# Unread TensorE products in the planner's gaps ahead of the first MoE, and four results in other rings

## The chip, the cores and the metric

The kernel runs on one core of one Trainium2 chip. The metric is the device time of one execution in microseconds; a run's figure is that of the core, and versions are compared by the median of several runs.

## The reference, cut to what matters

Three stages are computed one after the other, all in single precision.

```python
scores = where(causal, -1e9, q @ k.T / 8 + minimum(cum_k - cum_q, 0))   # 4 batches, 8 heads, 576 tokens, 64 wide
x = (exp(scores - max) / sum) @ v            # laid out as 2304 tokens x 512
h = x @ w_in                                 # 512 x 2048
x = (h * sigmoid(1.702 * h)) @ w_out         # 2048 x 512, the first MoE
P = balanced gate probabilities of x         # 8 experts, 8 rounds of row and column scaling
out = sum over e of P[:, e] * (relu(x @ w1[e]) @ w2[e])   # the second MoE, 1024 wide
```

Nothing that the change adds is part of this: its extra products are written to a PSUM tile that no instruction reads.

## The kernel before, in words

**Stages.** The attention works on 64 pieces, each a part of the queries of one head: scores (`sp` tiles), exponentials (`sm`), transposes (`tp`), a copy of the transposed probabilities (`pf`, later `ph` and `pl`), products with the values (`op`), and a division into token rows (`xg`), which are transposed again (`xtp`) into the input of the first MoE (`xh`, `xl`). Meanwhile the weights of the first MoE arrive in chunks (`st`), which ScalarE, GpSimd and VectorE turn into two parts each. The first MoE takes seven blocks of 256 tokens (`mm1`, `mm2`) and, at its end, the last two blocks together, 512 wide (`wide1`, `wide2`, lines 1174 to 1217): for every 128 of the 2048 hidden features, 12 products into `hp`, a tanh into `t`, a product by VectorE, a split into `gh` and `gl`, and 12 products into four accumulators `accw`. The second MoE follows with its experts.

**The rings.** `t`, `gh` and `gl` are rings of two buffers each in one pool (`mpool`). The same pool has a ring `st` of two larger buffers, the stages: `staged` (line 1398) hands them out to the early conversion of the second MoE's weights and of the first two x blocks (`early_x_part`, line 1490, names `xa` and `xb`). At the end of the first MoE, `wide2` scales the four accumulators into `xo` with ScalarE, takes the largest magnitude of each with VectorE, and sends each to DRAM (`x2_d`) by the SP queue. Before the change two buffers of the stages hold the four results, two in each.

**The planner.** The order of all instructions on all queues is not written out by hand. A planner in the kernel's own code (`Sequencer`, from line 61) keeps a clock for each engine, reckons a cost for every operation and a landing time for every transfer, and emits the instructions in the order in which they would run by that reckoning. Operations of TensorE are issued at once; those of the other engines are held until the planner's clock of TensorE reaches the time at which they could start, and then issued by rank, attention first and weight chunks last.

The loop from line 2104 makes one choice per pass. It asks six candidates when they could start: scaling of the values, a transpose of finished tokens, a value product, a transpose of probabilities, a score, the next piece of the first MoE. The first that could start now is emitted. If none could, the planner's clock of TensorE is set on, to the earliest of the six times or by 100 ns, whichever is less, and nothing is emitted.

**Unread products.** `fill(n)` (line 524) emits a product of n columns into the tile `unread`. At the start 14 of 512 columns are emitted (line 1937). Until the first piece of the first MoE (`at_first`, cleared in line 2039) there is also a rule on the share of busy time: `share()` (line 283) adds up what the planner has put on TensorE in the last stretch of its clock, of the constant length `WINDOW`, where products with single-precision stationary operands count for 0.36 of their cost, and divides by `WINDOW`. As long as that is under the constant `SHARE`, a product of 128 columns is emitted and the pass ends there, whether or not a candidate could have started. The planner reckons such a product at 128 / 2.4 + 2.7 = 56 ns. All operations are issued from line 357, so the profile's rows have that line and are told apart by their tiles; `unread<-mask` are the unread products.

Of the kernel before, what the change touches and what calls it, by code (L numbers as in the profile page):

```python
# [9 lines left out]
F32 = mybir.dt.float32  # L10
F32R = mybir.dt.float32r
# [18 lines left out]
def f32(ap):  # L30
    return ap.bitcast(F32)
# [9 lines left out]
SHARE = 0.55  # L41
# [357 lines left out]
def kernel(  # L399
# [12 lines left out]
    seq = Sequencer()  # L412
# [10 lines left out]
    TB1 = 256  # L423
# [33 lines left out]
    mpool = Pool(seq, p1.enter_context(tc.tile_pool(name="mpool", bufs=2, side=left, reuse_waits="tile")))  # L457
# [252 lines left out]
    def load_more():  # L710
        nonlocal n_qk
        while n_qk < min(len(heads), n_scored + 3 + N_KF if n_qk < H else n_prep + (3 if n_qk < 2 * H else 1)):
            if n_qk == H and n_s < 3 or n_qk == H + 2 and (n_s < 4 or auxpool.held()):
                return
            seq.rank = 1 if n_qk > 1 else 0
            load_qk(n_qk)
            n_qk += 1
            seq.rank = 1
            prep_next(n_scored)
            seq.rank = 0  # L720
# [93 lines left out]
    def can_vpow():  # L814
        if not vpows or n_s < 2:
            return never
        return max(seq.settled(vpows[0][1].tensor.name), seq.slot(ps_a, bank_tag("T")))
# [10 lines left out]
    def more_vpow():  # L828

        if due and not any(in_mpool(c) for c in range(n_conv, n_load)):  # L830
            begin_vpow(due.pop(0), 0, 3, 1)

    def more_v():

        nonlocal n_pv
        seq.rank = 1 if n_v else 0
        while n_pv < min(len(heads), (units[n_v][0] if n_v < NU else 0) + 2):
            b, h = extent(n_pv)[0:2]
            if n_pv < N_F:
                v3_of[n_pv] = [x[:, h] for x in (vf if n_pv >= H else vf[0:2])]  # L840
                n_pv += 1
                continue
            if (b, h) not in scaled:
                break
            if n_pv not in va_of:
                load_v(n_pv)
            prep_v(n_pv)
            n_pv += 1
            load_v(n_pv)
        seq.rank = 0  # L850
# [201 lines left out]
    def can_turn():  # L1052
        if n_t >= n_s or n_t >= n_v + 2:
            return never
        return max(seq.slot(ps_a, bank_tag("T")), seq.settled(live[n_t][0].tensor.name))
# [27 lines left out]
    def try_finish():  # L1083

        nonlocal n_fin
        while n_fin < len(heads) and (n_v == NU or units[n_v][0] > n_fin):
            g, h = heads[n_fin]
            if h == 0:
                olds = xgs.get(g - 1, [])[:1] + (xgs.get(g - 2, [])[1:] if g % 2 else [])
                if any(x[0].tensor.name == o.tensor.name for q in pieces.values() for x in q for o in olds):  # L1090
                    return
            finish(n_fin)
            n_fin += 1

    def can_flush():
        for j in (k for k in sorted(xtile) if k < NB1):
            if pieces[j]:
                return max(seq.slot(ps_a, bank_tag("T")), seq.settled(pieces[j][0][0].tensor.name))
        return never
# [91 lines left out]
    def wide2():  # L1191
        p, i, gh, gl = pend.pop(0)
        first, last = (p, i) == (NPAIR - 1, 0), (p, i) == (0, 1)
        if first:
            accs[NB1 - 1] = [
                pool.tile([128, 2, TB1], F32, tag=tag, name="accw")
                for pool, tag in ((ps_m, "acc0"), (ps_m, "acc1"), (mem["ps"], "D"), (mem["ps"], "E"))
            ]
        acc = accs[NB1 - 1]
        for m in range(KC):  # L1200
            d = slice(m * 128, (m + 1) * 128)
            for n, (w, x) in enumerate(((woh[p], gh), (woh[p], gl), (wol[p], gh))):
                nc.tensor.matmul(acc[m], lhsT=w[:, i, d], rhs=x, start=(first and n == 0), stop=(last and n == 2))
            if last:
                if m % 2 == 0:
                    both = staged("xo")
                xo = both[:, m % 2 * 512:m % 2 * 512 + 512].rearrange("p (a t) -> p a t", a=2)
                nc.scalar.activation(out=xo, in_=acc[m], func=ACTF.Copy, scale=0.5 / gain**2)
                c = 2 * (NB1 - 2) + m
                nc.vector.tensor_reduce(  # L1210
                    out=xmx[:, c:c + 1], in_=xo, axis=AX.XY, op=ALU.max, apply_absolute_value=True,
                )
                nc.sync.dma_start(
                    out=x2_d[-1][:, m, TB1:], in_=xo.rearrange("p a t -> p (a t)")
                )
# [17 lines left out]
    def convert():  # L1233

        nonlocal n_load, n_conv
        c = n_conv
        if c == len(chunks) or sum(x.rank == 2 for x in seq.held["DVE"]) > ASKED:
            return
        if n_s == 0:
            return  # L1240
        seq.rank = 2
        while n_load < len(chunks) and way(n_load)[0] is not None and way(n_load)[2] < c:
            conv_load(n_load)
            n_load += 1
        seq.rank = 0
        if c == 4 * NP0 and stage[0] is spool:
            if n_s < NU and units[n_s][0] < 2 * H - 2 or n_v < NU and units[n_v][0] < 2 * H - 2:
                return
            if min(n_pv, n_prep) < 2 * H or spool.held() or spool2[0].held():
                return  # L1250
            su.close()
            alloc_w(Pool(seq, p1b.enter_context(
                tc.tile_pool(name="wpool1", bufs=1, side=left, reuse_waits="tile")
            )), range(NP0, NP1))

            stage[0] = Pool(seq, su.enter_context(
                tc.tile_pool(name="stage", bufs=1, side=left, reuse_waits="tile")
            ))
        if c == 4 * NP1 and NP1 not in wih:
            if stage[0].held():  # L1260
                return
            su.close()
            alloc_w(Pool(seq, p1b.enter_context(
                tc.tile_pool(name="wpool2", bufs=1, side=left, reuse_waits="tile")
            )), range(NP1, NPAIR))
        seq.rank = 2
        conv(c)
        n_conv += 1
        seq.rank = 0
# [128 lines left out]
    def staged(name):  # L1398
        return mpool.tile([128, 1024], F32, tag="st", name=name, bufs=2)
# [676 lines left out]
    def more_scales():  # L2076
        nonlocal firsts, first_of
        if n_conv < len(chunks):
            return
        if firsts is None:  # L2080
            firsts = first_scales()
        elif first_of is None:
            return
        elif isinstance(first_of, int):
            if n_out < first_of:
                return
        elif first_of is vpows:
            if vpows:
                return
        elif seq.settled(first_of.tensor.name) > seq.free["PE"]:  # L2090
            return
        seq.rank = 2
        first_of = next(firsts, None)
        if hasattr(first_of, "send"):
            vpows.append((first_of, next(first_of)))
            first_of = vpows
        seq.rank = 0

    wgs = None
    at_first = [True]  # L2100
# [3 lines left out]
    while moe1_can is not None:  # L2104
        convert()
        try_finish()
        load_more()
        more_vpow()
        more_v()
        more_scales()  # L2110
        seq.run()
        now = seq.free["PE"]
        if not seq.rough and n_pv >= 2 * H:
            seq.rough = True
        for seq.slack in (0,) if seq.rough else (SLACK, 0):
            times = [can_vpow(), can_flush(), can_value(), can_turn(), can_score(), moe1_can()]
            which = next((k for k, x in enumerate(times) if x <= now), None)
        if at_first and seq.share() < SHARE:
            fill(128)
            continue  # L2120
            if which is not None:
                break
        seq.slack = 0
        if which is None:
            stuck += 1
            assert stuck < 3000
            seq.free["PE"] = min(min(times), now + 100)
            continue
        stuck = 0
        if which < 5:  # L2130
            (do_vpow, do_flush, do_value, do_turn, do_score)[which]()
        else:
            moe1_can = next(moe1, None)
# [4 lines left out]

    qs, pq = {}, {}
    wide2()  # L2140
    while first_of is not None:
        seq.free["PE"] += 100
# [155 lines left out]
    while upcoming or any(active):  # L2298
# [8 lines left out]
        now = seq.free["PE"]  # L2307
# [11 lines left out]
        if best is None:  # L2319
            t = min(t for _, t, _ in ready)  # L2320
# [62 lines left out]
```

## Time and profile before

| | us |
|---|---|
| median of 3 runs | 1974.06 |
| lowest and highest of them | 1973.75, 1977.65 |
| the profiled execution, device time | 1970.51 |
| its span, first to last instruction | 1968.8 |

The span is the time between the first and the last instruction of the profiled execution; its device time includes what lies around that. The profile's busy time of an engine counts the time in which an instruction of it runs. In the timeline a row is a merged run of like instructions: start, duration, engine, line, operation, tile written and tiles read, count, and in brackets the idle time before it and what ended that.

### The profile page before, as it was taken

The numbers are of one execution on the slowest core, as the hardware profiler recorded it, in microseconds if no ns is written. First come the engines' busy times: TensorE is split into PE (matmuls) and PEld (weight loads), VectorE is DVE, ScalarE is ACT, GpSimd is POOL, SyncE is SP. The second block draws the span as 40 slices with busy tenths as digits, with TensorE's granted clock in tenths as the row PEclk, the third lists the DMA queues.
The fourth block names the chain that finished last, engine by engine and source line by source line (L and its number), as shares of the span: only waits on it lengthen the run. The fifth ranks groups of instructions, "written<-read, shape, count | busy, mean of one in ns | idle before, by whom it ended". The sixth has DMA issues, their size and how long they took to land.

```text
span 1968.8 us, 41111 instructions
## 1 busy us (share of the span) xinstructions
PE 1948.9 (99%) x15766; PEld 1565.4 (80%) x15766; DVE 1477.7 (75%) x3424; ACT 1237.4 (63%) x2553; POOL 111.2 (6%) x174
## 2 busy tenths in 40 slices
PE   8999999999999999999999999999999999999999
PEld 6899999999987777777777777777777777777777
DVE  7997888887655787887868877766777877776556
ACT  6877676676545776665666766656666666665333
POOL 1120000000000000000010000111110000111000
PEclk9999999999999999999999999999999999999999
DMA  7564454443247653565575575576748547566331
GB/s 235 176 203 151 121 145 142 112 137 102 74 116 257 230 177 118 196 220 191 197 205 158 132 235 156 125 201 180 196 117 253 153 133 210 155 154 185 121 132 44
DMA packets 230101, 322.13 MB, mean 164 GB/s; under 512 B 38272, under 2 KB 156224, under 8 KB 229904
## 3 DMA queue, kind: packets, MB, share of 16 engines
q1 hardware_dynamic: 216944, 295.90, 46.1%
q0 software_dynamic: 12960, 23.60, 8.5%
q8 instruction: 124, 2.03, 0.4%
q14 instruction: 73, 0.60, 0.1%
HBM read 230.85 MB, written 84.34 MB: 160 GB/s over the span
## 4 chain that ended last, share of the span: by engine, by line
PE 83%; DVE 6%; ACT 5%; DMA 1%; issue 1%; SPq 0%; ACTq 0%; DVEq 0%
PE C L357 17%; PE A L357 16%; PE D L357 16%; PE hp L357 9%; PE B L357 8%; PE acc L357 6%; PE sp L357 2%; ACT h L357 2%; PE op L357 2%; PE tp L357 2%; PE accw L357 2%; DVE h L357 2%; PE accx L357 1%; DVE hst L357 1%; DVE sa L357 1%; ACT w1o L357 1%
## 5 line engine op out<-in xcount | busy, mean ns | idle before, releaser
L357 PEld LDWEIGHTS <-h 128*128 128x128 f16 x6048 | 591.6, 98 | 85.1 <-issue 6.9
L357 PEld LDWEIGHTS <-w1o 128*128 128x128 f16 x4036 | 394.5, 98 | 253.6 <-issue 2.5
L357 PE MATMUL C<-xt,w1o 128*128 128x384 f16 x1152 | 218.6, 326 | 1.2 <-DVE hst L357 1.2
L357 PE MATMUL D<-xt,w1o 128*128 128x384 f16 x1152 | 218.4, 326 | 0.0
L357 PE MATMUL D<-w2o,h 128*128 128x256 f16 x1728 | 217.5, 273 | 0.2 <-DMA xt<-xc_d 0.2
L357 PE MATMUL A<-xt,w1o 128*128 128x384 f16 x1152 | 214.5, 326 | 0.0
L357 PE MATMUL A<-w2o,h 128*128 128x256 f16 x1728 | 212.3, 273 | 1.9 <-ACT B L357 1.6
L357 PE MATMUL C<-w2o,h 128*128 128x256 f16 x1728 | 208.4, 273 | 1.7 <-DVE y L357 1.5
L357 DVE SCALAR_TENSOR_TENSOR h<-hst,h 128x768 f16<-128x768 f32 (+1 forms) x192 | 138.7, 752 | 56.6 <-ACT h L357 56.5
L357 ACT COPY C<-B 128x384 f32<-128x384 f32 (+1 forms) x168 | 71.4, 425 | 154.1 <-PE B L357 91.6
L357 PE MATMUL hp<-xh,wih 128*128 128x256 f32 (+1 forms) x512 | 154.6, 302 | 0.7 <-DVE t L357 0.7
L357 PE MATMUL hp<-xl,wih 128*128 128x256 f32 (+1 forms) x512 | 151.4, 296 | 0.0
L357 PE MATMUL hp<-xh,wil 128*128 128x256 f32 (+1 forms) x512 | 151.2, 295 | 0.0
L357 POOL DMA_DIRECT2D acc_d<-y x90 | 78.0, 867 | 1220.5 <-DVE y L357 660.8
L357 ACT ACTIVATE h<-hst 128x768 f16<-128x768 f32 (+1 forms) x192 | 126.3, 678 | 3.8 <-DVE hst L357 3.7
L357 ACT ACTIVATE sm<-sm,stats 64x576 f32<-64x576 f32 (+4 forms) x160 | 94.7, 603 | 40.9 <-DVE stats L357 39.4
L357 PE MATMUL acc<-gh,woh 128*128 128x256 f32 x384 | 111.4, 290 | 0.0
L357 PE MATMUL B<-w2o,h 128*128 128x256 f16 x864 | 110.3, 273 | 0.0
L357 PE MATMUL B<-xt,w1o 128*128 128x384 f16 x576 | 109.3, 326 | 0.0
L357 PE MATMUL acc<-gl,woh 128*128 128x256 f32 x384 | 108.4, 282 | 0.0
L357 PE MATMUL acc<-gh,wol 128*128 128x256 f32 x384 | 108.3, 282 | 0.0
L357 ACT COPY B<-A 128x384 f32<-128x384 f32 (+1 forms) x168 | 70.2, 425 | 60.2 <-PE A L357 59.6
(239 smaller groups left out, 3865.7 us busy)
## 6 DMA issues: line engine op xcount, KB each, us to landing
xt<-xc_d SPq DMA_DIRECT2D x168, 384.0 KB
wm<-in_moe_w_dram SPq DMA_DIRECT2D x112, 256.0 KB
w2o<-w_d SPq DMA_DIRECT2D x56, 512.0 KB
wr<-in_moe_w_dram SPq DMA_DIRECT2D x112, 256.0 KB
w_d<-wo SPq DMA_DIRECT2D x98, 256.0 KB
acc_d<-y POOLq DMA_DIRECT2D x90, 256.0 KB, 5.1
kq<-in_qk_dram SPq DMA_DIRECT2D x32, 448.0 KB
st<-in_moe_w_in_dram SPq DMA_DIRECT2D x16, 512.0 KB
```

The costliest lines, as they stand in the source:

```text
L357: self.seq.submit(self.name, what, lambda: method(*args, **named), outs, ins, "accum_op" in named)
```

## The change

The condition under which an unread product is emitted ahead of the first MoE gets a second case: no candidate could start now (`which is None`), and the earliest of the six times is more than 60 ns ahead. The old case stays. And the four results of the last two blocks no longer take the stages: the first two take buffers of the ring `t`, the third one of `gh`, the fourth one of `gl`, the latter two read and written as plain single precision. The lines after `continue` can't be reached, before or after.

```diff
@@ -1202,9 +1202,10 @@
             for n, (w, x) in enumerate(((woh[p], gh), (woh[p], gl), (wol[p], gh))):
                 nc.tensor.matmul(acc[m], lhsT=w[:, i, d], rhs=x, start=(first and n == 0), stop=(last and n == 2))
             if last:
-                if m % 2 == 0:
-                    both = staged("xo")
-                xo = both[:, m % 2 * 512:m % 2 * 512 + 512].rearrange("p (a t) -> p a t", a=2)
+                if m < 2:
+                    xo = mpool.tile([128, 2, TB1], F32, tag="t", name="xo", bufs=2)
+                else:
+                    xo = f32(mpool.tile([128, 2, TB1], F32R, tag=("gh", "gl")[m - 2], name="xo", bufs=2)[:, :, :])
                 nc.scalar.activation(out=xo, in_=acc[m], func=ACTF.Copy, scale=0.5 / gain**2)
                 c = 2 * (NB1 - 2) + m
                 nc.vector.tensor_reduce(
@@ -2115,7 +2116,7 @@
         for seq.slack in (0,) if seq.rough else (SLACK, 0):
             times = [can_vpow(), can_flush(), can_value(), can_turn(), can_score(), moe1_can()]
             which = next((k for k, x in enumerate(times) if x <= now), None)
-        if at_first and seq.share() < SHARE:
+        if at_first and (seq.share() < SHARE or which is None and min(times) > now + 60):
             fill(128)
             continue
             if which is not None:
```

## Rows read from the trace of the kernel before

**Rows 1.** The page, part 1: busy us, share of the span and count by engine.

```profile
PE 1948.9 (99%) x15766; PEld 1565.4 (80%) x15766; DVE 1477.7 (75%) x3424; ACT 1237.4 (63%) x2553; POOL 111.2 (6%) x174
```

**Rows 2.** Windows by stage: busy us (count) of PE, PEld, DVE, ACT, POOL; clock; DMA; GB/s.

```profile
2.40:43.26 40.86, 37.23 (x288) 29.21 (x288) 32.46 (x111) 25.94 (x53) 6.64 (x21) 1.00 0.87 255
43.26:633.00 589.74, 584.14 (x5202) 543.67 (x5201) 468.79 (x1385) 387.64 (x797) 24.82 (x54) 1.00 0.48 144
633.00:1940.00 1307.00, 1301.97 (x10052) 969.88 (x10052) 964.26 (x1907) 818.95 (x1697) 77.99 (x90) 1.00 0.58 172
```

**Rows 3.** Timeline of TensorE ahead of the first MoE: start, us, instruction, idle before.

```profile
9.84 0.92 PE L357 MATMUL sp<-kf 66*128 66x128 f32 x4 [0.21 <-DVE stats L357]
10.60 1.34 PE L357 MATMUL unread<-mask 128*128 128x128 bf16 x21
11.77 0.82 PE L357 MATMUL tp<-ident,sm 128*128 128x128 f32 x6
...
15.36 1.00 PE L357 MATMUL unread<-mask 128*128 128x128 bf16 x15
17.58 0.88 PE L357 MATMUL op<-vf,pf 128*128 128x65 f32 x6 [1.22 <-ACT pf L357]
...
21.14 0.88 PE L357 MATMUL op<-vf,pf 128*128 128x65 f32 x6 [0.70 <-ACT pf L357]
21.86 0.61 PE L357 MATMUL unread<-mask 128*128 128x128 bf16 x8
...
23.06 0.89 PE L357 MATMUL unread<-mask 128*128 128x128 bf16 x13
...
24.68 0.44 PE L357 MATMUL tp<-ident,sm 128*128 128x128 f32 x2 [0.30 <-DMA two<-one]
...
27.92 0.42 PE L357 MATMUL sp<-two 68*128 68x384 f32 x1 [0.63 <-DMA two<-aux_d]
...
29.25 0.44 PE L357 MATMUL unread<-mask 128*128 128x128 bf16 x5
29.90 0.35 PE L357 MATMUL sp<-one 128*64 128x288 f32 x1 [0.21 <-DVE stats L357]
...
35.55 0.67 PE L357 MATMUL unread<-mask 128*128 128x128 bf16 x9
36.39 1.05 PE L357 MATMUL tp<-ident,sm 64*128 64x64 f32 x8 [0.17 <-DVE xl L357]
37.28 0.22 PE L357 MATMUL unread<-mask 128*128 128x128 bf16 x1
```

**Rows 4.** Timeline of ScalarE, 16 to 21 us.

```profile
16.50 0.67 ACT L357 ACTIVATE st<-st 128x512 f32<-128x512 f32 x1 [0.65 <-DMA st<-in_moe_w_in_dram]
17.07 0.46 ACT L357 COPY pf<-tp 128x384 f32<-128x384 f32 x1
...
19.77 0.94 ACT L357 CAST one<-kq 128x896 fp32r<-128x896 f32 x1 [1.54 <-DMA kq<-in_qk_dram]
```

**Rows 5.** Timeline of TensorE at the first MoE's last unit.

```profile
630.31 0.50 PE L357 MATMUL accw<-gl,woh 128*128 128x512 f32 x1 [0.68 <-DVE gl L357]
630.64 0.40 PE L357 MATMUL accw<-gh,wol 128*128 128x512 f32 x1
```

**Rows 6.** Timelines of the SP queue, VectorE and ScalarE around the four results.

```profile
619.17 10.75 SPq L357 DMA_DIRECT2D xc_d<-xb  x7
...
629.57 0.68 DVE L357 TENSOR_TENSOR gl<-t,gh 128x512 fp32r<-128x512 f32 x1
...
631.08 2.65 ACT L357 ACTIVATE xo<-accw 128x512 f32<-128x512 f32 x4 [2.00 <-PE accw L357]
```

**Rows 7.** Windows of TensorE alone: length, busy us (count), granted clock, DMA share, GB/s.

```profile
2.40:8.15 5.75, 5.75 (x14) 1.00 0.40 113
...
17.00:18.00 1.00, 0.42 (x4) 1.00 0.79 269
18.00:25.00 7.00, 6.00 (x59) 1.00 1.01 271
```

## The prediction, made before the change was run

> **What bounds the kernel now.** I read the page's busy times first: TensorE is busy 99% of the span, VectorE 75% [rows 1]. So the end comes when TensorE has gone through its queue, and a change counts by what it takes out of or puts into that queue, products that nobody reads among it. The windows by stage say where TensorE is not busy. Ahead of the first product of the first MoE at 43.26 us it misses 40.86 - 37.23 = 3.63 us; in the 590 us of the first MoE 5.60 us and in the 1,307 us of the second 5.03 us [rows 2]. Then the timeline of TensorE ahead of 43.26 us: the unread products stand there in eight places, 14 of 512 columns at the start and 72 of 128 columns in seven runs of 21, 15, 8, 13, 5, 9 and 1 [rows 3]. They count as busy, but 21 of them take 11.77 - 10.60 = 1.17 us, 56 ns each, so 72 take 4.0 us. What follows a run tells what it costs: behind the runs of 15, 5 and 9 TensorE waits, for 1.22, 0.21 and 0.17 us, so the useful product could not have come sooner and these 29 cost nothing; behind those of 21, 8, 13 and 1 the next product starts at once, so these 43, 2.4 us, may hold work back. The third thing to see are the real waits between the useful products: 0.21 us at 9.84, 1.22 at 17.58, 0.70 at 21.14, 0.30 at 24.68, 0.63 at 27.92, 0.21 at 29.90 and 0.17 at 36.39, 3.44 us in all [rows 3].
>
> **Part one: products in the planner's gaps.** The edit adds a product of 56 ns wherever the planner sees nothing ready for more than 60 ns; since 56 is under 60, its own clock doesn't run past the time at which something becomes ready. So in the planner's reckoning nothing is late. Two things follow on the chip.
>
> First, products are added. How many, the trace doesn't say, since the planner's gaps aren't the chip's. The least is none. The most that the chip can hide is its whole idle time, 3.44 us, or 61 products. I leave out the two waits for ScalarE's copy of the probabilities (17.58 and 21.14), because that copy stood behind another operation of ScalarE which had waited for a load, 0.65 us for a weight chunk and 1.54 us for a head [rows 4]; I take the planner to reckon these loads as landed. The other five are the kind that it reckons too (VectorE's statistics, transfers that it costs): 0.21 + 0.30 + 0.63 + 0.21 + 0.17 = 1.52 us, or 27 products. I take 25, on the low side of the middle.
>
> Second, products are removed. Each added product stands in the same sum from which the share is formed, for as long as it is in the window, and so pays for one of the forced ones that come after it. That holds only if a forced run follows soon: 3 of the run at 10.60 after the wait at 9.84, the 5 at 29.25 after the wait at 27.92, the 1 at 37.28 after that at 36.39 [rows 3]. The other waits have no run close behind. So 9 of the 72 go.
>
> What of this reaches the end? The 25 added ones cost nothing as long as the chip waits where the planner does; the cover is the five waits above. If it is gone, 25 x 56 ns = 1.4 us is the price. Of the 9 that go, the 5 at 29.25 stand in front of a wait and are worth nothing; the 3 at 10.60 are worth 3 x 56 ns = 0.17 us, which runs into the wait of 1.22 us at 17.58 and is lost there; the 1 at 37.28 is worth 0.06 us. From 43.26 us on the first MoE has products for most gaps and TensorE is busy for 584.14 of 589.74 us [rows 2], so what is gained earlier is kept: **-0.1 us**. The ends are -2.4 us, if all 43 that hold work back go and nothing else is late, and +1.4 us.
>
> What the edit issues is TensorE work alone: no transfer, nothing on the queues of SP and POOL. But the planner decides everything else by its clock and by what is ready at each pass, so fewer forced products mean another order of transposes, scores, values and weight chunks on all queues. For this I have no row of its own. The bound is what order can touch: the 5.60 + 5.03 us of idle time behind 43.26 us [rows 2]. Order may take a third of it or add as much, 3.5 us either way; with no reason for a sign I take 0.
>
> **Part two: where the last four results go.** Before, they take the ring of the stages, whose tenants before them are the blocks of the early conversion of the second x block. If they had waited for it, ScalarE's operations would start late. They don't: their row names TensorE's products as what was waited for (2.00 us), the first starts at 631.08, where its last product, started at 630.64 with 0.40 us, ends at 631.04, and the four follow each other, 2.65 us in one piece [rows 5, 6]. The last transfers out of the ring's old tenant were issued by 629.92 [rows 6]. So there is nothing to win, and in the rings of the units nothing new to wait for: the results go to the places of the last unit but one and to the `t` of the last, all read by the time the last products run, since the last `gl` is done at 629.57 + 0.68 = 630.25 [rows 6]. The four operations, reductions and transfers stay. The second MoE's planner sees its ScalarE free a little sooner, which may exchange neighbours in its first units; that belongs to the order above. I put the part at **0**, between -0.7 us (the only wait of TensorE there, 0.68 us for `gl`, if the new order spared it) [rows 5] and +0.7 us for a second such wait.
>
> **The sum.** -0.1 + 0 (order) + 0 (part two) = -0.1 us. The profiled execution took 1970.51 us (span 1968.8 and 1.7 around it), so it would be 1970.4. The median of the runs shown is 3.55 us above that execution; the same step from it gives 1974.06 - 0.1 = **1974.0 us**. The measurement of this kernel can tell about 0.2% from no change, 3.9 us: its three runs alone are that far apart. So I expect no difference that shows.
>
> **The rivals.** (a) The forced products that hold work back all go, as the gaps' products keep the share over its limit, and the transposes, issued sooner, bring the probabilities to ScalarE ahead of the loads that it waits for, so that the waits at 17.58 and 21.14 go too. For it: the 21 at 10.60 are forced in front of transposes that then start without a wait. Against it: the gaps are short, and single-precision products still count for 0.36 of their time, so the share drops as before. It is 2.4 + 1.22 + 0.70 = 4.3 us: 1969.8 us.
>
> (b) The array's clock. The granted clock is 1.00 in all stretches [rows 2, 7], also where TensorE is busy for only 0.42 of 1 us [rows 7]. It says the same of the first 14 products, which took 5.75 / 14 = 0.41 us for 512 columns, the pace of the 1.2 GHz level, so I go by the pace of products. The 128 columns in 56 ns at 10.60 are that of 2.4 GHz, and behind the two longest waits it is the same: 13 unread products take 0.89 us at 23.06, 21 took 1.34 at 10.60, and the difference is 56 ns for each of the eight [rows 3]. So nothing is to be won in this execution. In the timed ones it could be otherwise, as they take 3.55 us more. If they fell to the lower level at the wait of 17.58 and stayed there until 25, the 6.00 us busy of 18 to 25 [rows 7] would take twice as long; less the 1.0 us idle there, 5.0 us go. The time would be 1969.1 us. The Trainium skill (TensorE: Matmul & The Clock Gate, section "HAM oscillation — how this bites in real kernels") says that waits between groups of products send the clock back to half rate; by that rule the edit would be worth rival (b), and the trace shown doesn't bear it out.
>
> (c) Slower, by ScalarE's queue. At 16.50 ScalarE begins an operation on a weight chunk after waiting 0.65 us for its load, the copy of the probabilities stands behind it, and TensorE waits 1.22 us for that copy [rows 3, 4]. Transfers are busy for 0.79 and 1.01 of the stretches from 17 to 25 us [rows 7], so no load comes sooner because a plan has it so. If the new plan, whose clock runs ahead of the chip, puts chunks ahead of copies more often, each such place costs 1.22 us. One more is hidden in the range; it decides from four on: 4 x 1.22 = 4.9 us less 0.1, 1978.9 us. Against it: chunks are issued last in rank, and only one place of the kind stands in the trace.
>
> (d) The change does nothing: the planner finds hardly a gap of over 60 ns, and the ring was never waited for. Time 1974.1 us.
>
> **How the numbers follow.** Forecast 0.50, (d) 0.08, (a) 0.13, (b) 0.11, (c) 0.18. Forecast and (d) are within 0.2%: 0.58. (a) and (b) are faster by more: 0.24; (c) is slower by more: 0.18. The range runs from just under (a) to (c)'s four places, 1969.5 to 1978.9: the forecast with the 3.5 us of order and the 1.4 us of uncovered products (1970.5 to 1978.9 at most) lies in it; what is left out is most of (b) and the longer forms of (c).
>
> **What would show it.** Right: the runs of unread products at 10.60, 29.25 and 37.28 are shorter, new ones stand where there are waits at 9.84, 24.68, 27.92 and 29.90, the first MoE begins within 1 us of 43.26, and the four results still start as their products end. Wrong: unread products well over 72 + 25 with useful ones late behind them; the first MoE begins 3 us sooner (a) or later (c); a timed median 5 us lower with nothing earlier in the trace (b); or a difference that arises only behind 43.26 us, which would be the order that I put at 0.

## The result, and the profile after

The changed kernel takes 1986.97 us (median of 4 runs, 1984.59 to 1989.09), beside 1974.34 us before (4 runs): a ratio of 1.0066 [1.005, 1.0083], slower by 12.6 us. The forecast was no change, 1974.0 us, and the time lies above its range of 1969.5 to 1978.9. The profiled execution took 1984.59 us with a span of 1982.8, 14.0 us more than the span of before.

Page, part 1, of the changed kernel, which answers to [rows 1]:

```profile
PE 1953.8 (99%) x15765; PEld 1569.9 (79%) x15765; DVE 1477.5 (75%) x3424; ACT 1238.1 (62%) x2553; POOL 110.3 (6%) x174
```

TensorE is still what bounds the kernel, but two things grew: its busy time by 4.9 us, with one product less, and its idle time (span less busy) from 19.9 to 29.0 us, by 9.1. The windows of TensorE say where. First before, then after (length, busy us and count, granted clock, DMA share, GB/s):

```profile
2.40:200.00 197.60, 191.89 (x1721) 1.00 0.63 193
200.00:633.00 433.00, 429.48 (x3767) 1.00 0.45 131
633.00:700.00 67.00, 66.38 (x588) 1.00 0.65 226
...
```

```profile
2.40:200.00 197.60, 183.24 (x1582) 0.97 0.63 193
200.00:633.00 433.00, 432.02 (x3858) 1.00 0.44 127
633.00:700.00 67.00, 63.25 (x479) 1.00 0.64 223
...
```

Length less busy is TensorE's idle time. Up to 200 us TensorE idles for 197.60 - 183.24 = 14.36 us where it idled for 5.71, 8.7 more, and its granted clock is 0.97; from 200 to 633 it idles 2.5 us less, and at the seam of the two MoEs, 633 to 700, 3.1 us more. From 700 to 1940 us nothing changed (1235.59 us busy before, 1235.70 after).

TensorE's timeline of the changed kernel ahead of the first MoE, which answers to [rows 3]:

```profile
...
18.11 0.85 PE L357 MATMUL op<-vf,pf 128*128 128x65 f32 x6 [1.60 <-ACT sm L357]
18.80 0.89 PE L357 MATMUL unread<-mask 128*128 128x128 bf16 x13
23.37 1.00 PE L357 MATMUL unread<-mask 128*128 128x128 bf16 x15
...
28.35 0.41 PE L357 MATMUL sp<-two 68*128 68x384 f32 x1 [1.60 <-DMA two<-aux_d]
32.18 1.08 PE L357 MATMUL unread<-mask 128*128 128x128 bf16 x8
37.87 0.56 PE L357 MATMUL unread<-mask 128*128 128x128 bf16 x7
...
40.53 0.28 PE L357 MATMUL hp<-xh,wih 128*128 128x256 f32 x1
```

In eleven runs (4, 2, 2, 7, 2, 6, 13, 15, 5, 8 and 7, of which four are shown) there are 71 products of 128 columns, one fewer than before: the kernel of e4, below, issues 47 in all, the forced ones, in runs of 2, 2, 7, 2, 6, 13 and 15, so the runs of 4, 5, 8 and 7 (at 8.63, 25.80, 32.18 and 37.87 us) are the 24 new ones, and 25 of the old ones are gone. The first MoE begins at 40.53 instead of 43.26 us. Of these 2.73 us, 0.83 are the first 14 products, which took 5.75 us before [rows 7] and take 4.92 after. The last product of the first MoE, before and then after:

```profile
632.70 0.39 PE L357 MATMUL accw<-gh,wol 128*128 128x512 f32 x1
```

```profile
643.83 0.39 PE L357 MATMUL accw<-gh,wol 128*128 128x512 f32 x1
```

It begins 2.73 us sooner and ends 11.1 us later, at 644.2 instead of 633.1.

**The clock.** TensorE in three windows of the changed kernel:

```profile
30.00:34.00 4.00, 4.00 (x27) 0.57 0.98 378
54.00:58.00 4.00, 4.00 (x22) 0.57 0.14 43
98.00:102.00 4.00, 3.37 (x32) 0.57 0.46 117
```

At a granted clock of 0.57 in the mean the 11.37 us busy cost, as an estimate, 0.43 x 11.37 = 4.9 us, as much as the busy time grew. (The first 14 products took 0.83 us less, so about as much growth elsewhere isn't traced.) Before, the clock is 1.00 in all of these. Each of the three stands behind waits: 1.60 us at 28.35 (above), 1.39 at 52.22, and four from 94.77 to 98.31, the first of 0.92 us (both below).

The order of before isn't free of such falls. Two experiments below, e2 and e3, have that order, and in their profiled executions TensorE has these windows, e2 first:

```profile
30.00:34.00 4.00, 4.00 (x18) 0.50 1.02 402
```

```profile
26.00:30.00 4.00, 4.00 (x18) 0.50 0.97 273
```

So part of the 4.9 us is that the one profiled execution of before had no fall. In the three with its order TensorE is busy for 1948.9 to 1951.5 us and idle for 19.9 to 20.4; in the three with the order of the changed kernel (after, e1, e4) it is busy for 1953.8 to 1957.9 and idle for 26.3 to 29.0.

**The waits up to 100 us.** TensorE's timeline of the changed kernel, its longer waits between 43 and 100 us:

```profile
48.91 0.85 PE L357 MATMUL op<-vf,pf 128*128 128x65 f32 x6 [0.34 <-ACT wih L357]
52.22 1.08 PE L357 MATMUL op<-vf,pf 128*128 128x65 f32 x8 [1.39 <-DVE vd L357]
...
61.47 1.08 PE L357 MATMUL op<-vf,pf 128*128 128x65 f32 x8 [0.59 <-DVE xgl L357]
70.35 1.08 PE L357 MATMUL op<-vf,pf 128*128 128x65 f32 x8 [0.55 <-ACT woh L357]
...
94.77 0.22 PE L357 MATMUL op<-v,ph 128*128 128x65 f16 x2 [0.92 <-DVE xg L357]
```

All are value products, 3.8 us in all. They write into one of two places of `op`, which VectorE must have read for the head before the last (`stats<-op`, `xg<-op`, `xgl<-op`). The releasers named differ, since other operations end at about the same time, but each of the first four products begins 0.14 or 0.15 us after such a reading ends. VectorE's timeline ahead of the wait at 61.47:

```profile
59.54 0.14 DVE L357 TENSOR_SCALAR stats<-op 64x1 f32<-64x1 f32 x1
59.60 0.67 DVE L357 SCALAR_TENSOR_TENSOR t<-st 128x512 int32<-128x512 int32 x1
...
60.29 0.65 DVE L357 SCALAR_TENSOR_TENSOR t<-st 128x512 int32<-128x512 int32 x1
60.91 0.29 DVE L357 SCALAR_TENSOR_TENSOR xg<-op,stats 128x128 f32<-128x128 f32 x1
61.12 0.20 DVE L357 SCALAR_TENSOR_TENSOR xgl<-op,stats 64x64 f32<-64x64 f32 x1
```

Two operations on weight chunks (`t<-st`, 0.67 and 0.65 us) stand between the head's statistics and its division. Without them the division would be free some 1.3 us sooner, more than the 0.59 us that the product waits. The others are less plain: at 52.22, 70.35 and 94.77 one chunk operation (0.69, 0.67 and 0.69 us) stands there, beside operations of the first MoE and of the attention, and at 48.91 VectorE had itself waited 0.63 us for TensorE. The wait of 1.60 us at 18.11 is of this kind too, though ScalarE is named: the product begins 0.16 us after VectorE's reading ends, and that stood behind a chunk operation which had waited 1.13 us for GpSimd's part of the chunk. VectorE's timeline:

```profile
17.20 0.69 DVE L357 SCALAR_TENSOR_TENSOR t<-st 128x512 int32<-128x512 int32 x1 [1.13 <-POOL st L357]
17.80 0.15 DVE L357 TENSOR_SCALAR stats<-op 128x2 f32<-128x2 f32 x1
```

**The seam.** ScalarE's and TensorE's timelines of the changed kernel, which answer to [rows 6]:

```profile
642.93 1.24 ACT L357 ACTIVATE xo<-accw 128x512 f32<-128x512 f32 x2 [0.15 <-PE accw L357]
644.06 0.34 ACT L357 CAST xb<-xa 128x192 f16<-128x192 f32 x1
644.30 0.60 ACT L357 ACTIVATE xo<-accw 128x512 f32<-128x512 f32 x1
647.38 0.30 ACT L357 ACTIVATE lt<-gp,ig 128x48 f32<-128x48 f32 x1 [2.48 <-DVE ig L357]
```

```profile
647.73 1.05 PE L357 MATMUL gp<-wgs,xt 128*128 128x16 f16 x36 [1.49 <-ACT lt L357]
...
661.09 1.14 PE L357 MATMUL C<-xt,w1o 128*128 128x384 f16 x6 [1.14 <-ACT C L357]
```

Before, the early conversion of x was through by 629.92 [rows 6]. Now it reaches into the four results: `xb` stands between the third and the fourth, and the last transfer out of it, on the SP queue, is issued from 645.54 on. A scale that the second MoE's gate needs (`ig`, by VectorE) comes late, ScalarE's operation on the gate's products (`lt<-gp,ig`) behind it, and TensorE waits 1.49 us, later 1.14.

### The profile page after: what moved, and what is told of

Its sections match the earlier page's. It is cut to its first block, busy times and chain, and to the rows that moved or that the text cites. A ratio compares the mean times of both kernels' runs of the same rounds, so it can differ in the third digit from the quotient of the medians.

```text
span 1982.8 us, 41124 instructions
## 1 busy us (share of the span) xinstructions
PE 1953.8 (99%) x15765; PEld 1569.9 (79%) x15765; DVE 1477.5 (75%) x3424; ACT 1238.1 (62%) x2553; POOL 110.3 (6%) x174
## 4 chain that ended last, share of the span: by engine, by line
PE 57%; ACT 5%; DVE 4%; DMA 0%; issue 0%; SPq 0%; ACTq 0%
PE C L357 16%; PE A L357 16%; PE D L357 16%; PE B L357 8%; ACT h L357 2%; DVE h L357 2%; DVE hst L357 1%; DVE sa L357 1%; ACT w1o L357 1%; ACT hst L357 1%; DVE sb L357 1%; DMA xr<-x_d 0%; ACT B L357 0%; ACT C L357 0%; ACT m L357 0%
```

## The experiments

All times are medians of timed runs beside runs of the kernel before on the same chip. The kernels differ in order, in unread products and in where results are kept.

| kernel | us | before | ratio |
|---|---|---|---|
| e1 gap products alone | 1988.78 | 1972.41 | 1.0080 [1.0061, 1.0100] |
| e2 rings alone | 1972.27 | 1972.41 | 0.9999 [0.9990, 1.0008] |
| e3 products outside the plan, order of before | 1971.94 | 1972.41 | 0.9993 [0.9984, 1.0003] |
| e4 order of after, no gap products | 1986.13 | 1972.41 | 1.0066 [1.0047, 1.0085] |
| e5 before, SHARE 0.50 | 1976.35 | 1972.40 | 1.0018 [1.0009, 1.0028] |
| e6 before, SHARE 0.60 | 1991.14 | 1972.40 | 1.0095 [1.0080, 1.0110] |
| e7 gap products left out of the share | 1992.57 | 1972.40 | 1.0105 [1.0090, 1.0120] |
| e8 after, chunks reckoned 2 us later | 1990.25 | 1972.40 | 1.0087 [1.0070, 1.0104] |
| e9 after, second expert begun at the seam | 1985.80 | 1972.10 | 1.0069 [1.0054, 1.0084] |
| e10 the same on e7 | 1985.52 | 1972.10 | 1.0068 [1.0053, 1.0083] |
| e11 after, products in two waits | 1986.21 | 1972.10 | 1.0077 [1.0060, 1.0094] |
| e12 before, chunks reckoned 0.1 us later | 1992.03 | 1972.97 | 1.0092 [1.0077, 1.0107] |
| e13 after, gaps over 300 ns only | 1981.72 | 1972.97 | 1.0045 [1.0028, 1.0062] |

### Which part: e1 to e4

e1 has the new condition alone, e2 the new places of the results alone, both as in the diff of the change. e3 keeps the order of before and puts products into the planner's gaps behind its back:

```diff
+            covered = max(covered, now)
+            while at_first and covered + 60 < seq.free["PE"]:
+                tc.nc.tensor.matmul(unread[:, 0:128], ...)
+                covered += 56
```

e4 keeps the order of after: its gap products are reckoned, but not issued.

```diff
-            fill(128)
+            if seq.share() < SHARE:
+                fill(128)
+            else:
+                seq.submit("PE", "matmul", lambda: None, [unread[:, 0:128]], ...)
```

> Part one alone: the second case of the condition, with the four results in the stages as before. Theory order (the products count in the share and on the planner's clock, so that the planner emits everything else in another order, in which TensorE runs ahead of transfers and waits): most of the loss stays, +8 to +13 us on before, with stretches of granted clock under 1 in the first 110 us as in the changed kernel. Theory rings (the loss comes from where the four results go): within 2 us of before. The first 640 us should be those of the changed kernel, its end of the first MoE at about 644 us.

> Part two alone: the four results in the units' rings, no product added. Theory rings: +3 us on before, since in the changed kernel TensorE waits 3.75 us between 633 and 700 us against 0.62 before. Theory order: those waits belong to the order that part one led to, so this is within 1 us of before. The first 630 us are those of before.

> The kernel before, with the products emitted in the planner's gaps but neither counted in the share nor on the planner's clock: the order of all other instructions is that of before. Theory products (they stand in front of useful work): +1 to +2 us. Theory order: within 1 us of before, first MoE begins at 43 to 44 us, granted clock 1.00 throughout.

> The changed kernel's order with the products of the second case left out of the program: the planner reckons them as if they were there. They are written to a tile that nobody reads. Theory order: as slow as the changed kernel or slower, 1985 to 1992 us, with the granted clock under 1 in as many stretches or more. Theory products: back to within 2 us of before.

e2 is worth nothing in the order of before. e3 has 12 products in gaps beside the 72 forced ones, and by the interval they cost at most 0.0003 x 1972 = 0.6 us. Part of its expectation failed: the clock fell at 26 us (above), and the first MoE begins at 45.49 us, as it does at 45.85 in e2, so its start differs by over 2 us between executions of one order. e1 loses 16.4 us, more than the 8 to 13 expected and, by the intervals, no more than the whole change. In its order the stages aren't free: ScalarE's first two results wait for the conversion `xb`, and TensorE waits 3.42 us for them.

```profile
647.51 1.08 ACT L357 ACTIVATE xo<-accw 128x512 f32<-128x512 f32 x2 [2.95 <-DVE xb L357]
```

The changed kernel has no such wait, but the times of the two don't tell whether that gains anything. e4, which multiplies nothing in the gaps, loses as much as the whole change. Windows of TensorE of e4:

```profile
2.40:200.00 197.60, 184.53 (x1545) 0.94 0.60 190
...
633.00:700.00 67.00, 64.71 (x475) 0.97 0.65 224
```

The same places as after: 13.07 us idle up to 200, a clock of 0.94 there, 2.29 us idle at the seam. So the loss comes with the order alone.

### Which order: e5 to e8, e12 and e13

e5 and e6 change one constant of the kernel before (SHARE 0.55 to 0.50 and 0.60). e7 takes the gap products out of the sum of the share (`if not forced: seq.streams.pop()`), so that 95 unread products of 128 columns are issued. e8 and e12 reckon the landing of the weight chunks later, by 2 us in the changed kernel and by 0.1 us in the kernel before:

```diff
+        seq.late = CHUNK_LATE
         ...
         nc.sync.dma_start(out=st, in_=src)
+        seq.late = 0.0
```

e13 is the changed kernel with 300 in place of 60 ns. The "first expert" of the expectations is the first MoE.

> The kernel before with the share at which products are forced lowered from 0.55 to 0.50, nothing else: no product in gaps, results in the stages; the planner gets another order because fewer products are forced. Theory any order (the order of before is a good one among many, and nearly any change of it costs as much): +6 to +15 us on before, with waits of TensorE of 4 us or more between 43 and 200 us. Theory gaps (products in gaps in particular lead to a bad order, by letting TensorE run ahead): within 3 us of before or, as fewer products are forced here too, at most half of the loss.

> The kernel before with the share raised from 0.55 to 0.60, nothing else: more products are forced, so TensorE runs ahead of transfers less. Theory any order: +6 to +15 us on before. Theory ahead (the loss comes from TensorE running ahead of ScalarE and transfers, since fewer products hold it back): within 3 us of before, on either side, with the first MoE beginning later than 43 us.

> The changed kernel, but the products in gaps are taken out of the sum from which the share is formed: they stay on the planner's clock and in the program, and about as many products are forced as before. Theory count (the loss comes from the forced products that they replace, 25 of 72): within 2 us of before. Theory any order: slower than before by 6 us or more, since the order is still not that of before.

> The changed kernel, with the loads of the first MoE's weight chunks reckoned as landing 2 us later, so that the planner puts the chunks' operations on ScalarE and VectorE behind copies of probabilities that it put in front of them. Theory chunks (TensorE's waits at 42.9, 52.2 and 70.4 us come from such copies standing behind chunks): 3 to 8 us faster than the changed kernel, those waits gone. Theory any order: no faster than the changed kernel by more than 3 us, other waits in their place.

> The kernel before with no product added and no ring changed; the planner only reckons the loads of the weight chunks 0.1 us later, which gives another order. Theory any order (the order of before is a favourable one, and most others cost 4 us or more): 1976 or more, ratio 1.002 to 1.010. Rival (the loss is of the order that the gap products make: TensorE's share of unread products is reached earlier and the first expert starts earlier): within 0.2% of before.

> The changed kernel, with an unread product only where the planner has nothing ready within 300 ns (60 in the change): fewer gap products, more forced ones left, another order again. Theory any order: not the changed kernel's time cut in proportion, anything between before and 1.0% above it, with the lost time again as TensorE's waits by 200 us, the granted clock behind them, and the seam. Rival (the loss goes with the number of gap products): a ratio of 1.002 to 1.004, and a first expert that starts at about 42 us.

e5 loses 3.95 us: less than the 6 of "any order", and within the "at most half of the loss" of the theory of gaps, so it speaks for the latter. e6 loses 18.7 us, more than the 6 to 15, though its first MoE begins at 50.31 us, and e7 20.2 us: "any order" has the sign of both, "ahead" and "count" have neither.

e12 decides that no product in a gap is needed. It puts none there, changes a reckoned time by 0.1 us, and loses 19 us, no less than the change did. Windows of TensorE of e12, and its ScalarE and TensorE at the seam:

```profile
2.40:200.00 197.60, 188.90 (x1629) 0.96 0.61 191
...
633.00:700.00 67.00, 53.06 (x391) 0.90 0.56 191
```

```profile
646.99 0.93 ACT L358 ACTIVATE xa<-xa,sc 128x768 f32<-128x768 f32 x1 [5.97 <-DMA xa<-x_d]
...
654.63 0.30 ACT L358 ACTIVATE lt<-gp,ig 128x48 f32<-128x48 f32 x1 [0.64 <-DVE ig L358]
```

```profile
654.98 1.11 PE L358 MATMUL gp<-wgs,xt 128*128 128x16 f16 x36 [12.77 <-ACT lt L358]
```

Here a block of x is still to be loaded when the first MoE ends, and its whole conversion stands in front of the gate: 12.77 us of TensorE's time. The same wait for `lt` is 10.71 us in e6, 11.22 in e7 and 11.11 in e8. So orders lose in different places: e12 idles for 13.9 us at the seam and 8.7 up to 200, the changed kernel for 3.75 and 14.4. Up to 200 us the three executions with the order of before idle for 5.7 to 6.6 us, e5 to e8, e12 and e13 for 8.0 to 10.5, and the order of the changed kernel (after, e1, e4) for 13.1 to 14.4: any other order lost something there, and that of the change the most.

Part of the expectation of e8 was met. Its window of TensorE from 43 to 100 us, and its wait for the gate:

```profile
43.26:100.00 56.74, 53.06 (x458) 0.90 0.56 171
```

```profile
653.55 1.11 PE L358 MATMUL gp<-wgs,xt 128*128 128x16 f16 x36 [11.11 <-ACT lt L358]
```

With the chunks later, the waits of value products between 43.26 and 100 us are 0.28, 0.17 and 0.44 us (at 64.92, 70.24 and 89.32) in place of the 3.8 us above, and TensorE idles for 56.74 - 53.06 = 3.68 us there, where the changed kernel has 6.38. That fits the reading that chunks ahead of the divisions make these waits. But the wait ahead of 42.9 us stayed (0.82 us at 42.94), a new one of 1.44 us stands at 97.76, the clock fell all the same (0.90), and the seam took 11 us: the time went the other way.

e13: up to 23 us its unread runs in TensorE's timeline (21, 15, 8, 13) are those of before, and behind them stand runs of 7, 4 and 2 where before has 5, 9 and 1 [rows 3]. That is enough for 1.0045 [1.0028, 1.0062], with the changed kernel's waits at the seam (1.5 and 1.1 us). Its ratio alone doesn't tell the theories apart, as the interval holds the rival's upper figure, and the first MoE begins at 40.5 us and not at 42. Seven orders other than that of before were run here (after with e1 and e4, e5, e6, e7, e8, e12, e13); all are slower, by 4 to 20 us. Three of them, e5, e6 and e12, have no product in a gap.

### The seam: e9 and e10

A call is moved from the moment the second MoE's first weights are begun to just behind the seam, in the changed kernel (e9) and in e7 (e10):

```diff
-        second_expert()
 ...
+    second_expert()
```

The call doesn't issue the conversion of a block, as the expectations say, but what the scales of the weights of the second MoE's second expert need: 16 loads and 16 operations `wm<-wm` of ScalarE. In the changed kernel the last of these stands in the middle of the conversion of x, and in e9 the first stands behind the seam. ScalarE's timeline of the changed kernel and then of e9:

```profile
640.54 0.63 ACT L357 ACTIVATE wm<-wm 128x512 f32<-128x512 f32 x1
```

```profile
688.62 0.63 ACT L357 ACTIVATE wm<-wm 128x512 f32<-128x512 f32 x1
```

> The changed kernel, with the start of the second expert's early work (conversion of its first block) moved from the moment its first weights are begun to just behind the seam of the two experts. Theory seam (part of the loss is the conversion still standing ahead of the gate when the first expert ends, 1.5 + 1.1 us of TensorE's waits at 647 to 661 us): 1.5 to 2.6 us less than the changed kernel, ratio to before about 1.005. Rival (the work has only been moved, and the gate waits for it anyway): within 1 us of the changed kernel, or slower.

> The same move on the kernel of e7 (gap products left out of the share), where the gate waited 11.2 us for the conversion. Theory seam: the wait goes, about 10 us less than e7 (1992.6), near 1983. Rival (another piece of the second expert's work is late instead): the idle time turns up within 20 us of the seam and the total stays within 2 us of e7.

Rows of TensorE's timeline, its wait for the gate in e7 and then in e10:

```profile
656.97 1.11 PE L357 MATMUL gp<-wgs,xt 128*128 128x16 f16 x36 [11.22 <-ACT lt L357]
```

```profile
644.88 1.11 PE L357 MATMUL gp<-wgs,xt 128*128 128x16 f16 x36 [3.12 <-ACT lt L357]
```

The wait falls by 8.1 us and the ratio from 1.0105 to 1.0068, which is 0.0037 x 1972 = 7.3 us. That is less than the 10 expected, as 3.12 us of the wait stay, but TensorE's idle time from 633 to 700 us falls from 11.6 to 4.1 us, so the seam's part is shown for e7. In e9 the wait is gone as well (66.51 of 67.00 us busy at the seam), and still the ratio is 1.0069, as that of the changed kernel. Its gain, 1.5 to 2.6 us expected, is 0.08 to 0.13% and smaller than either interval: for the changed kernel the seam's price is read from the trace, and not confirmed by the times.

### The clock: e11

Unread products, put in outside the plan, fill the two waits at 28.35 and 52.22 us:

```diff
+                    if x is not xs[0]:
+                        hold(HOLD_S.pop((n, qb), 0))
...
+        hold(HOLD_V.get((n, u[0]), 0))
...
+    HOLD_V = {(10, 3): 22}
+    HOLD_S = {(8, 2): 26}
```

> The changed kernel, with 26 unread products put outside the plan in front of the score product that waits for a DMA at 28.35 us (1.60 us) and 22 in front of the value product that waits at 52.22 us (1.39 us), so that TensorE multiplies during these two waits. Theory clock (each of the two waits is followed by some 3.3 us at about half the clock): the granted clock stays near 1.00 in 30 to 34 and 54 to 58 us, and the time is 2 to 3.5 us less than the changed kernel's. Rival (the clock has other causes): the two dips stay, the time is within 1 us of the changed kernel's.

Windows of TensorE of e11:

```profile
30.00:34.00 4.00, 3.74 (x36) 1.00 1.03 395
54.00:58.00 4.00, 3.65 (x34) 1.00 0.31 92
94.00:102.00 8.00, 7.28 (x56) 0.57 0.26 69
160.00:172.00 12.00, 11.19 (x83) 0.72 0.61 192
```

Both dips are gone, and the value product that began at 52.22 begins at 50.44, 1.78 us sooner. But the dip behind 94 us is 8 us long and another stands at 160 to 172, where the changed kernel has a clock of 1.00; the last product of the first MoE starts at 643.42 instead of 643.83, so 0.4 us of the 1.8 are left, and the times show nothing: 1.0077 [1.006, 1.0094]. These two dips needn't come of the filling: e1 and e4, in the same order and with nothing filled, have them too. TensorE in e1 and then in e4:

```profile
166.00:170.00 4.00, 3.58 (x16) 0.57 0.37 113
```

```profile
166.00:170.00 4.00, 4.00 (x32) 0.60 0.68 188
```

So the clock falls behind waits, as the theory has it, and filling the two kept it up there; that this lowers the time isn't shown. The rival's condition (the dips stay) isn't met, though its time is.

## Why the prediction was wrong

**The bound: right.** TensorE's queue sets the end, before and after; the 14.0 us between the two profiled executions are its idle time (9.1) and its busy time (4.9), the latter about what the clock costs.

**Products added: right in price, and in number by luck.** 25 were predicted, 24 came. But the 25 were worked out from five waits of the order of before, at 9.84 and 24.68 to 36.39 us; the 24 stand in four runs of another order. They come at no cost that shows, by e3 with 12 in the order of before, and by e4, which leaves the 24 out without a gain.

**Products removed: wrong.** 9 forced ones were to go, 25 went. The prediction held that a gap's product pays only where a forced run follows soon. The trace after has the runs in other places altogether, and the first MoE at 40.53 us, not within 1 us of 43.26 (a sign too fine in any case, as e2 and e3 begin at 45.85 and 45.49 in the order of before). Nor was what is gained earlier kept: 2.73 us sooner at the start of the first MoE, 11.1 us later at its end.

**Part two: right in the order of before.** Nothing, by e2. That the stages are free held for that order alone, as e1 shows.

**Order: the step that failed.** It was "with no reason for a sign I take 0", within 3.5 us, where the change of order cost 12.6. The bound was worked out from the 5.60 + 5.03 us of idle time that there were behind 43.26 us [rows 2]. Idle time that is there bounds only what a new order can win. What it can lose isn't bounded by it: a chunk put ahead of a division, a conversion not finished at the seam, a clock that falls behind the new waits are times that the trace of before doesn't hold. And there was a reason for a sign: the order of before idles for 19.9 us in 1,968.8, so another one has more to lose than to win. The seven other orders that were run say so, e12 most plainly.

**Rival (c)** had the right sign and a mechanism of the right kind on the wrong queue. Its own waits, of value products for ScalarE's copies, shrank: 0.37 us at 24.74 after, 1.22 and 0.70 before. Weight chunks do stand ahead of what TensorE waits for, but on VectorE, ahead of its readings of `op`: at 18.11, and in four of the five waits shown between 43 and 100 us. From 43 to 100 us the five make 3.8 us (rows above), where before has one of the kind, of 0.37 us, at 46.42: 3.4 of the 8.7 us lost up to 200. It wasn't alone: the clock and the seam are no part of it. That the chunks are the cause of these waits is read from the trace and fits e8, but isn't shown: no kernel was run in which only VectorE's queue differs; the remaining idle time up to 200 us wasn't traced to single choices of the planner and stays open.

**Rival (b)** had the right resource and the wrong sign. That the clock falls in some executions of before, as it supposed, is so: their mean clock is 0.997 to 1.000, and the windows of e2 and e3 show such falls. But the change made them more and not fewer: the four runs of the changed kernel have 0.991 to 0.997. The rule of the Trainium skill (TensorE: Matmul & The Clock Gate, section "HAM oscillation — how this bites in real kernels"), that waits between groups of products send the clock back to half rate, is borne out by the trace after in the three windows shown, and not behind every wait, as the last section says. The prediction used it only for what the added products might win, and not for the waits that a new order may make.

**Rivals (a) and (d)** fell. In (a) all 43 forced products that hold work back go and the time falls by 4.3 us; 25 went and it rose. In (d) hardly a product is added; 24 were.

## What to carry to other kernels

An edit that feeds a planner is an edit of the whole schedule: price it first as a draw among orders, and test that by a change of the planner's input that does no work (here 0.1 us on one landing time, which cost 19 us). If the present order leaves the bounding engine almost no idle time, the draw is likelier to lose than to win (here seven of seven lost), and the idle time that is there is no bound on the loss. To use idle time without this risk, add the work behind the planner's back and leave its reckoning as it is; that cost nothing measurable here (e3), though it won nothing that could be measured either.

## What the runs showed of the hardware

In the dip at 54 us the first MoE's products of 256 columns follow each other every 0.21 us, behind it every 0.12. But the granted clock doesn't fall behind every wait of one length. Behind the wait of 1.60 us at 18.11 the changed kernel has a clock of 1.00 up to 30 us, behind that of 1.60 us at 28.35 it is 0.57 from 30 to 34. Nor does one order decide it: between 160 and 172 us it fell in e1, e4 and e11, where the changed kernel, with 5.99 of 8 us busy from 160 to 168, kept 1.00. What decides between these wasn't found. A dip costs little, as an estimate 0.43 x 4 = 1.7 us for 4 us at 0.57, but it comes on top of the wait that it follows.
